# Two heads' attention scores side by side in the matmul array, in two passes

## The chip, the cores and the metric

The kernel runs on one core of one Trainium2 chip. The metric is device time in microseconds of one execution. A core has five engines with queues of their own: PE (TensorE, the 128 x 128 matmul array, whose weight loads the profile lists as PEld), DVE (VectorE), ACT (ScalarE), POOL (GpSimd) and SP (SyncE, which here only issues DMAs). Engines wait for one another through semaphores. Matmuls write to PSUM, which the kernel uses as eight banks of 128 x 512 float32.

## The reference

The input has 2048 tokens of 448 numbers, 16 heads of 28. Two attention layers work on the same input, and a gate per token mixes them. Layer A is linear attention with learned features. Layer B is full softmax attention, and its core is what the change touches:

```python
scores = jnp.einsum("bhqd,bhkd->bhqk", q, k) * scale
p = _softmax(scores, axis=-1)
o = jnp.einsum("bhqk,bhkd->bhqd", p, v)
...
return g * a + (1 - g) * b
```

## The kernel before

Layer A and all projections fill the first third of the time. The change lies in the rest, the attention of layer B from line 810 on.

**Precision.** Queries and keys are each split into a high part, rounded to the format F32R, and a low part, what the rounding left (`keep_qk`, line 568). Both lie in DRAM. A score is the sum of four products: high with high, high with low, low with high, low with low.

**Stacks.** `load_stack` (line 822) lays these parts over the 128 rows of a tile in four blocks of 32 rows. For queries the blocks hold the parts high, high, low, low; for keys high, low, high, low. One matmul over 128 rows then gives all four products at once. A tile has four heads side by side along its columns, so a stack is 128 x 4 x 512. Each block's rows 4 to 31 hold the 28 numbers of a head. Row 0 is used for the maximum: keys have −1 there, queries the row maximum of the scores (`load_nm`, line 832), so that the matmul gives score minus maximum, and ScalarE can take the exponential directly. There are two query stacks and five key stacks; `stack` (line 815) fills them once on POOL.

**Steps.** Heads come in four groups g of four, queries in four blocks qb of 512, keys in 16 tiles kt of 128. The loop from line 1094 makes 256 steps s, 16 for each pair of g and qb. A step has, in this order on PE:

- `scores(s, 0)` and `scores(s, 1)` (line 844): four matmuls st, one for each head, into a PSUM bank each; ScalarE makes p = exp(st) from each (line 868)
- `values(s - 1)` (line 970): the product of the p of the step before with the values, in four column strips of 32 (eight matmul instructions, pv)
- `mx_visit()` (line 304): a visit of the search for row maxima of later blocks. Four matmuls pm on 28 rows each, in four row strips; ScalarE copies one of them (rl, line 325) and frees its bank, DVE reduces the others (lines 329 and 332)

The visits end after about 212 steps. From then on a block also has four projections of finished output (`project`, line 982).

**Banks.** One bank belongs to pv; seven go round in the list `free`. After the scores, line 872 puts the banks back in an order that mixes those that ScalarE empties with those that DVE empties. The bank of rl goes in last (line 916), and so the fourth score of the next step takes it.

**DMA.** The order on PE, DVE, ACT and POOL is that of the program. SP's order is set by a scheduler. At kt = 12 of a block the program loads queries and maxima of the next (lines 1103 to 1106), and new keys in the last block of a group. `finish` (line 1014) normalizes a block: the denominators go out to DRAM and back (denb, rdb, rsb), POOL multiplies, and the result is stored (od). In the last block `load_out` (line 930) reads into a key stack that is no longer used.

Of the kernel before, what the change touches and what calls it, by code (L numbers as in the profile page):

```python
# [9 lines left out]
F32R = mybir.dt.float32r  # L10
# [7 lines left out]
P = 128  # L18
# [3 lines left out]
DH = 28  # L22
GW = 112
NG = 4
# [10 lines left out]
def f32(ap):  # L35
    return ap.bitcast(F32)
# [3 lines left out]
def gated_mix_kernel(ctx, tc, xT, wqkB, wvB, wvA, wkAT, wqAT, phi, woA, woB,  # L40
# [7 lines left out]
    nc = tc.nc  # L48
# [18 lines left out]
    def ps_mx(nm, d):  # L67
        return ps.tile([P, 2, 512], F32, tag="md" if d and psn[1] == 3 else "mx", name=nm,
                       bufs=1 if d and psn[1] == 3 else 2)
# [6 lines left out]
    q_d = [qk_d[g * GW:(g + 1) * GW] for g in range(NG)]  # L76
    k_d = [qk_d[D + g * GW:D + (g + 1) * GW] for g in range(NG)]
# [628 lines left out]
    for i in range(2 * NT + 11):  # L706
        t, q = i, i - NT
# [102 lines left out]
    at = ctx.enter_context(tc.tile_pool(name="at", bufs=1, side="right", reuse_waits="tile"))  # L810
    qst_of, kst_of = {}, {}
# [1 line left out]


    def stack(nm, keys):
        r = at.tile([P, 4, 512], F32R, name=nm)
        nc.gpsimd.memset(f32(r), 0.0)
        if keys:
            nc.gpsimd.memset(f32(r[0:1]), -1.0)
        return r  # L820

    def load_stack(r, src, c, parts):
        for b, i in enumerate(parts):
            nc.sync.dma_start(f32(r[32 * b + 4:32 * b + 32]),
                              src[:, i, c:c + 512].rearrange("(j d) n -> d j n", d=DH))
        return r

    def load_q(gq):
        g, qb = divmod(gq, NQ)
        qst_of[gq] = load_stack(qst[gq % 2], q_d[g], qb * 512, (0, 0, 1, 1))  # L830

    def load_nm(gq):
        nm = nm_of.pop(gq)
        row = f32(qst_of[gq][0:1].rearrange("p a (t b r) -> p (a t) b r", b=4, r=32))
        for b in range(4):
            nc.sync.dma_start(row[:, :, b, :], nm[32 * b:32 * b + 16, :])

    def load_k(g, kb):
        kst_of[(g, kb)] = load_stack(kst[(4 * g + kb) % 5], k_d[g], kb * 512, (0, 1, 0, 1))

    NS = NG * NQ * NT
    pv_of, pts, late, mids = {}, {}, {}, {}
# [1 line left out]
    def scores(s, i):  # L844

        gq, kt = divmod(s, NT)
        g, qb = divmod(gq, NQ)

        def score(j, st):
            nc.tensor.matmul(st, kst_of[(g, kt // 4)][:, j, (kt % 4) * P:(kt % 4 + 1) * P],  # L850
                             qst_of[gq][:, j, :], start=True, stop=True)

        if s == 0:
            p = at.tile([P, 2, 512], F32, name=f"p{s}_{i}")
            st = ps_mx(f"st{s}_{i}", i)
            for jl in range(2):
                score(2 * i + jl, st[:, jl, :])
            nc.scalar.activation(p, st, AF.Exp, scale=SCALE)
            pts.setdefault(s, []).extend([p[:, 0, :], p[:, 1, :]])
            return  # L860
        sts = []
        for j in (2 * i, 2 * i + 1):
            used.append(free.pop(0))
            sts.append(bank(used[-1], f"st{s}_{j}"))
            score(j, sts[-1])
        for st in sts:
            p = late_p.tile([P, 512], F32, tag="p", name=f"p{s}_{len(pts.get(s, []))}", bufs=8)
            nc.scalar.activation(p, st, AF.Exp, scale=SCALE)  # L868
            pts.setdefault(s, []).append(p)
        if i == 1:  # L870
            a, m = used[:], held[:]
            free.extend([a[0], m[0], a[1], m[1], a[2], a[3], m[2]] if m else a)
            used.clear()
            held.clear()

    qst = [stack("qst0", False)]
    kst = [stack(f"kst{i}", True) for i in range(5)]
    qst.append(stack("qst1", False))
    stg = at
    load_q(0)  # L880
    load_nm(0)
    ps_s_.close()
    ps = ps_s_.enter_context(tc.tile_pool(name="psv", bufs=1, space=PSUM, reuse_waits="tile"))
# [4 lines left out]
    for t in range(8, NT):  # L888


        if t < NT - 1:
            value_b(t, lambda i: mx_unit() if (11 * (t - 8) + i + 1) * rest // 77
                    > (11 * (t - 8) + i) * rest // 77 else None)
        else:
            value_b(t, lambda i: scores(0, i // 3 - 1) if i in (4, 7) else None)
        take_acts()
        if t in (8, 12):
            load_k(0, t // 12)
# [12 lines left out]
    def bank(i, nm):  # L911
        return ps2.tile([P, 512], F32, tag=f"g{i}", name=nm, bufs=1)
# [17 lines left out]
    def load_out(qb):  # L930


        if qb < NQ - 1:
            o = late_p.tile([P, NG - 1, 2, 512], F32R, tag="oL", name=f"oL{qb}", bufs=1)
            oL_of[qb] = [o[:, b] for b in range(NG - 1)]
        else:
            o = kst[(4 * NG) % 5]
            oL_of[qb] = [o[:, 0:2], o[:, 2:4],
                         late_p.tile([P, 2, 512], F32R, tag="oLl", name="oLl", bufs=1)]
        tt = slice(qb * 512, (qb + 1) * 512)  # L940
        for b in range(2):
            nc.sync.dma_start(f32(oL_of[qb][b]), o_d[b * P:(b + 1) * P, :, tt])
        r = oL_of[qb][2]
        for i in range(2):
            nc.sync.dma_start(f32(r[:80, i, :]), o_d[256:336, 0, tt])
        nc.sync.dma_start(f32(r[80:, 0, :]), o_d[288:336, 1, tt])
        nc.sync.dma_start(f32(r[80:96, 1, :]), o_d[288:304, 1, tt])
        nc.sync.dma_start(f32(r[96:, 1, :]), o_d[256:288, 1, tt])
# [145 lines left out]
    for s in range(NS + 16):  # L1094
        take_acts()
        if s < NS:
            gq, kt = divmod(s, NT)
            g, qb = divmod(gq, NQ)
            if s in (0, 3):
                load_k(0, 2 + s // 3)  # L1100
            if g + 1 < NG and qb == NQ - 1 and kt % 4 == 2:
                load_k(g + 1, kt // 4)
            if kt == 12 and gq + 1 < NG * NQ:
                load_q(gq + 1)
            if kt == (12 if gq + 1 < 14 else 14) and gq + 1 < NG * NQ - 1:
                load_nm(gq + 1)
            if s in OUTS:
                load_out(OUTS.index(s))
            if g == NG - 1 and kt == 8:
                load_acc(qb)  # L1110
            if s:
                scores(s, 0)
                scores(s, 1)
# [15 lines left out]
        if NG * NQ - 1 in nm_of and NG * NQ - 1 in qst_of:  # L1129
            load_nm(NG * NQ - 1)  # L1130
# [70 lines left out]
```

## Time and profile before

| what | value |
|---|---|
| runs | 1028.19 and 1028.88 us, median 1028.54 |
| span of the profiled execution | 1027.1 us |
| its own time | one of the two runs, 1.1 or 1.8 us over the span |
| PE busy | 1018.7 us, 99% |
| ACT busy | 819.4 us, 80% |
| DVE busy | 672.8 us, 65% |
| st matmuls | 1024, 315.6 us busy |
| pv matmuls | 2048, 272.8 us busy |
| pm matmuls in visits | 848, 107.1 us busy |
| DMA queue of the program | 97.74 MB, 35.4% of 16 engines |
| clock granted to PE | 0.998 of full |

The span runs from the first to the last instruction of the core. "Busy" is the union of an engine's instructions. Matmuls are pipelined: the next one begins before the one before has ended, so durations of neighbours overlap: what a matmul costs is the distance between starts. The same holds for ScalarE. In the timeline a row gives start, length, engine, line, operation, tiles and count, with merged neighbours in one row, and in brackets the idle time before it and what ended it.

### The profile page before, as it was taken

The numbers are of one execution on the slowest core, as the hardware profiler recorded it, in microseconds if no ns is written. First come the engines' busy times: TensorE is split into PE (matmuls) and PEld (weight loads), VectorE is DVE, ScalarE is ACT, GpSimd is POOL, SyncE is SP. The second block draws the span as 40 slices with busy tenths as digits, with TensorE's granted clock in tenths as the row PEclk, the third lists the DMA queues.
The fourth block names the chain that finished last, engine by engine and source line by source line (L and its number), as shares of the span: only waits on it lengthen the run. The fifth ranks groups of instructions, "written<-read, shape, count | busy, mean of one in ns | idle before, by whom it ended". The sixth has DMA issues, their size and how long they took to land.

```text
span 1027.1 us, 17751 instructions
## 1 busy us (share of the span) xinstructions
PE 1018.7 (99%) x6344; PEld 561.2 (55%) x6344; DVE 672.8 (65%) x1335; ACT 819.4 (80%) x1534; POOL 245.1 (24%) x213
## 2 busy tenths in 40 slices
PE   8999999999999999999999999999999999999998
PEld 7878888878779433333333333333333333354545
DVE  5466566997750578888878788787878887710102
ACT  5354445687753899999999999999999999969672
POOL 1226456688436302111011110101201101011010
PEclk9999999999999999999999999999999999999999
DMA  8873110132245703233633123522313355414311
GB/s 294 292 243 116 42 34 19 43 90 79 91 129 122 158 19 83 65 71 68 127 70 77 46 66 81 129 57 50 87 46 74 87 131 138 124 56 127 122 42 54
DMA packets 64025, 98.88 MB, mean 96 GB/s; under 512 B 17952, under 2 KB 24720, under 8 KB 63936
## 3 DMA queue, kind: packets, MB, share of 16 engines
q1 hardware_dynamic: 63936, 97.74, 35.4%
q8 instruction: 50, 0.82, 0.4%
q14 instruction: 39, 0.32, 0.1%
HBM read 69.54 MB, written 27.78 MB: 95 GB/s over the span
## 4 chain that ended last, share of the span: by engine, by line
PE 95%; DVE 2%; DMA 1%; ACT 1%; issue 0%; SPq 0%; DVEq 0%; ACTq 0%
PE st L850 29%; PE pv L977 25%; PE pm L321 9%; PE pqk L108 5%; PE poa L108 4%; PE pk L126 4%; PE pva L126 4%; PE pob L108 3%; PE pq L108 3%; PE pvb L108 2%; PE pmb L284 2%; PE pvb L126 2%; PE pn L532 1%; PE pft L520 1%; PE pkv L475 1%; PE poL L1011 1%
## 5 line engine op out<-in xcount | busy, mean ns | idle before, releaser
L868 ACT ACTIVATE p<-st 128x512 f32<-128x512 f32 x1020 | 525.9, 609 | 29.5 <-PE st L850 27.8
L332 DVE TENSOR_REDUCE part<-pm 128x1 f32<-128x512 f32 x477 | 304.6, 685 | 131.5 <-PE pm L321 124.9
L850 PE MATMUL st<-qst,kst 128*128 128x512 f32 x1024 | 315.6, 430 | 0.5 <-ACT vb L694 0.5
L977 PE MATMUL pv<-p,vb 128*32 128x512 f32 x2048 | 272.8, 605 | 0.2 <-DVE oUb L398 0.2
L850 PEld LDWEIGHTS st<-qst,kst 128*128 128x128 f32 x1024 | 173.1, 187 | 137.4 <-issue 75.8
L321 PEld LDWEIGHTS pm<-kc,qc 28*128 28x128 f32 x848 | 40.5, 181 | 177.8 <-ACT p L868 169.4
L325 ACT ACTIVATE rl<-pm 128x512 f32<-128x512 f32 x212 | 126.9, 599 | 11.1 <-PE pm L321 0.3
L419 POOL TENSOR_TENSOR oUb<-oUb,rsb 128x512 f32<-128x512 f32 x15 | 19.4, 1291 | 469.2 <-DMA rsb<-rdb 375.1
L329 DVE CUSTOM_DVE_ANT_0 rl<-pm,rl 128x512 f32<-128x512 f32 x159 | 108.2, 680 | 0.0
L321 PE MATMUL pm<-kc,qc 28*128 28x512 f32 x848 | 107.1, 495 | 0.0
L289 DVE CUSTOM_DVE_ANT_0 rl<-pmb,rl 128x512 f32<-128x512 f32 x88 | 57.1, 686 | 32.4 <-ACT rl L287 32.4
L977 PEld LDWEIGHTS pv<-p,vb 128*32 128x32 f32 x2048 | 40.3, 108 | 67.6 <-issue 63.4
L988 DVE SCALAR_TENSOR_TENSOR acc<-pob,gate,acc 128x448 f32<-128x448 f32 x12 | 8.2, 683 | 86.2 <-PE pob L108 86.2
L108 PE MATMUL pqk<-XH,wB 128*128 128x512 f32 x192 | 60.8, 404 | 2.3 <-DVE ev L572 2.3
L287 ACT ACTIVATE rl<-pmd 128x1024 f32<-128x1024 f32 x44 | 45.3, 1029 | 8.0 <-ACT z_s L485 2.4
L571 ACT CAST ev<-pqk 128x512 fp32r<-128x512 f32 x28 | 16.0, 589 | 40.2 <-PE pqk L108 35.7
L108 PE MATMUL poa<-woA_s,oTa 128*128 128x448 f32 x192 | 43.2, 374 | 0.0
L108 PEld LDWEIGHTS pqk<-XH,wB 128*128 128x128 f32 x192 | 36.0, 192 | 11.4 <-DVE ev L572 2.7
L572 DVE TENSOR_TENSOR ev<-pqk,ev 128x512 fp32r<-128x512 f32 x28 | 19.0, 690 | 31.6 <-ACT ev L571 31.5
L108 PEld LDWEIGHTS poa<-woA_s,oTa 128*128 128x128 f32 x192 | 35.0, 188 | 5.8 <-issue 2.8
L195 POOL TENSOR_TENSOR kc<-kc,kd 28x512 fp32r<-28x512 f32 x12 | 15.4, 1282 | 95.7 <-DMA kc<-qkd 59.4
L126 PE MATMUL pk<-wkA_s,XH 128*128 128x448 f32 x128 | 37.9, 377 | 0.0
(155 smaller groups left out, 1186.6 us busy)
## 6 DMA issues: line engine op xcount, KB each, us to landing
qkd<-ev SPq DMA_DIRECT2D x28, 512.0 KB
qst<-qkd SPq DMA_DIRECT2D x64, 224.0 KB
kst<-qkd SPq DMA_DIRECT2D x64, 224.0 KB
od<-oTb SPq DMA_DIRECT2D x48, 112.0 KB
rsa<-rda SPq DMA_DIRECT2D x8, 512.0 KB
rsb<-rdb SPq DMA_DIRECT2D x15, 256.0 KB
kc<-qkd SPq DMA_DIRECT2D x64, 56.0 KB
gad<-ga SPq DMA_DIRECT2D x16, 224.0 KB
```

Source lines behind the costliest of these rows:

```text
L108: nc.tensor.matmul(dst, l, r, start=i == 0, stop=i == len(todo) - 1)
L126: nc.tensor.matmul(dst[:, :n], l, r, start=i == 0, stop=i == len(todo) - 1, skip_group_check=True)
L284: nc.tensor.matmul((pb if j < 2 else pd)[:, j % 2, :], qc[js, qt * P:(qt + 1) * P], kc[js, :], start=True, stop=True, tile_position=(32 * ...
L287: nc.scalar.activation(rl, pd, AF.Relu)
L289: nc.vector.tensor_tensor_reduce(rl[:, i, :], pb[:, i, :], rl[:, i, :], 1.0, LOWEST, ALU.add, ALU.max, part[:, col + i:col + i + 1])
L321: nc.tensor.matmul(pm[j], mxs[("qc", gq)][js, qt * P:(qt + 1) * P], mxs[("kc", g, kb)][js, :], start=True, stop=True, tile_position=(32 * ...
L325: nc.scalar.activation(rl, pm[kb], AF.Relu if kb < 3 else AF.Copy)
L329: nc.vector.tensor_tensor_reduce(r, pm[j], r, 1.0, LOWEST, ALU.add, ALU.max, part[:, col + j:col + j + 1])
L332: nc.vector.tensor_reduce(part[:, col + j:col + j + 1], pm[j], AX.X, ALU.max)
L850: nc.tensor.matmul(st, kst_of[(g, kt // 4)][:, j, (kt % 4) * P:(kt % 4 + 1) * P], qst_of[gq][:, j, :], start=True, stop=True)
L868: nc.scalar.activation(p, st, AF.Exp, scale=SCALE)
L977: nc.tensor.matmul(pv[32 * j:32 * j + 32, :], vb[kt // 8][:, kt % 8, 4 * g + j, :], pt[j], start=kt == 0, stop=kt == NT - 1, tile_position ...
```

## The change

The array is split into two halves of 64 rows, and two heads work at the same time, one in each half. The blocks of 32 rows now hold, for keys: high and low part of the pair's first head, high and low part of its second. For queries all four blocks hold one part, and a second set of columns the other: `[:, pair, 0, :]` has the high parts and `[:, pair, 1, :]` the low ones. A score is the sum of two passes, high then low part of the queries, against the same keys, accumulated in the head's bank. A pair is issued as: pass 0 of both heads, pass 1 of both heads.

So a step has eight score matmuls on 64 rows for four on 128, each with its own weight load. Key stacks shrink from 128 x 4 x 512 to 128 x 2 x 512, query stacks keep their size. Keys are loaded with as many DMAs as before, of half the size; queries with eight DMAs for four, of half the size each; the maxima with sixteen DMAs of 4 rows for four DMAs of 16, since they now go to row 0 and row 64 and to pass 0 alone. ScalarE's reads of a pair follow both of its passes. The last block's output has a tile of its own in place of a key stack.

```diff
     def stack(nm, keys):
-        r = at.tile([P, 4, 512], F32R, name=nm)
+        r = at.tile([P, 2, 512] if keys else [P, 2, 2, 512], F32R, name=nm)
         nc.gpsimd.memset(f32(r), 0.0)
         if keys:
-            nc.gpsimd.memset(f32(r[0:1]), -1.0)
+            for e in (0, 64):
+                nc.gpsimd.memset(f32(r[e:e + 1]), -1.0)
         return r
...
+    def half(src, i, c, e):
+        return src[:, i, c:c + 512].rearrange("(p e d) n -> e d p n", e=2, d=DH)[e]

     def load_q(gq):
         g, qb = divmod(gq, NQ)
-        qst_of[gq] = load_stack(qst[gq % 2], q_d[g], qb * 512, (0, 0, 1, 1))
+        qst_of[gq] = r = qst[gq % 2]
+        for b in range(4):
+            for i in range(2):
+                nc.sync.dma_start(f32(r[32 * b + 4:32 * b + 32, :, i, :]),
+                                  half(q_d[g], i, qb * 512, b // 2))

     def load_nm(gq):
         nm = nm_of.pop(gq)
-        row = f32(qst_of[gq][0:1].rearrange("p a (t b r) -> p (a t) b r", b=4, r=32))
+        for e in range(2):
+            for p in range(2):
+                row = f32(qst_of[gq][64 * e:64 * e + 1, p, 0, :]).rearrange(
+                    "o (t b r) -> o t b r", b=4, r=32)
+                for b in range(4):
+                    at_row = 32 * b + 8 * p + 4 * e
+                    nc.sync.dma_start(row[:, :, b, :], nm[at_row:at_row + 4, :])
+
+    def load_k(g, kb):
+        kst_of[(g, kb)] = r = kst[(4 * g + kb) % 5]
         for b in range(4):
-            nc.sync.dma_start(row[:, :, b, :], nm[32 * b:32 * b + 16, :])
-
-    def load_k(g, kb):
-        kst_of[(g, kb)] = load_stack(kst[(4 * g + kb) % 5], k_d[g], kb * 512, (0, 1, 0, 1))
+            nc.sync.dma_start(f32(r[32 * b + 4:32 * b + 32]),
+                              half(k_d[g], b % 2, kb * 512, b // 2))
...
-        def score(j, st):
-            nc.tensor.matmul(st, kst_of[(g, kt // 4)][:, j, (kt % 4) * P:(kt % 4 + 1) * P],
-                             qst_of[gq][:, j, :], start=True, stop=True)
+        def pair(sts):
+            for x in range(2):
+                for e in range(2):
+                    rows = slice(64 * e, 64 * e + 64)
+                    nc.tensor.matmul(
+                        sts[e], kst_of[(g, kt // 4)][rows, i, (kt % 4) * P:(kt % 4 + 1) * P],
+                        qst_of[gq][rows, i, x, :], start=x == 0, stop=x == 1,
+                        tile_position=(64 * e, 0), skip_group_check=True)
...
         for j in (2 * i, 2 * i + 1):
             used.append(free.pop(0))
             sts.append(bank(used[-1], f"st{s}_{j}"))
-            score(j, sts[-1])
+        pair(sts)
...
-            o = kst[(4 * NG) % 5]
+            o = at.tile([P, 4, 512], F32R, name="oLs")
```

More of the change, by code (lines that the diff above doesn't have):

```diff
@@ L815, in stack @@
     def stack(nm, keys):
-        r = at.tile([P, 4, 512], F32R, name=nm)
+        r = at.tile([P, 2, 512] if keys else [P, 2, 2, 512], F32R, name=nm)
         nc.gpsimd.memset(f32(r), 0.0)
         if keys:
-            nc.gpsimd.memset(f32(r[0:1]), -1.0)
-        return r
[L822 to L826, printed above, removed]
+            for e in (0, 64):
+                nc.gpsimd.memset(f32(r[e:e + 1]), -1.0)
+        return r
+    def half(src, i, c, e):
+        return src[:, i, c:c + 512].rearrange("(p e d) n -> e d p n", e=2, d=DH)[e]
     def load_q(gq):
         g, qb = divmod(gq, NQ)
-        qst_of[gq] = load_stack(qst[gq % 2], q_d[g], qb * 512, (0, 0, 1, 1))
+        qst_of[gq] = r = qst[gq % 2]
[3 more added lines that the diff above has]
+                                  half(q_d[g], i, qb * 512, b // 2))
     def load_nm(gq):
         nm = nm_of.pop(gq)
-        row = f32(qst_of[gq][0:1].rearrange("p a (t b r) -> p (a t) b r", b=4, r=32))
+        for e in range(2):
[7 more added lines that the diff above has]
+        kst_of[(g, kb)] = r = kst[(4 * g + kb) % 5]
         for b in range(4):
-            nc.sync.dma_start(row[:, :, b, :], nm[32 * b:32 * b + 16, :])
-    def load_k(g, kb):
-        kst_of[(g, kb)] = load_stack(kst[(4 * g + kb) % 5], k_d[g], kb * 512, (0, 1, 0, 1))
+            nc.sync.dma_start(f32(r[32 * b + 4:32 * b + 32]),
+                              half(k_d[g], b % 2, kb * 512, b // 2))
     NS = NG * NQ * NT
@@ L855, in scores @@
             st = ps_mx(f"st{s}_{i}", i)
-            for jl in range(2):
-                score(2 * i + jl, st[:, jl, :])
+            pair([st[:, jl, :] for jl in range(2)])
             nc.scalar.activation(p, st, AF.Exp, scale=SCALE)
```

## The prediction

> **What bounds the kernel now.** I read the page first, for the engine that carries the end.
>
> ```profile
> span 1027.1 us, 17751 instructions
> ...
> PE 1018.7 (99%) x6344; PEld 561.2 (55%) x6344; DVE 672.8 (65%) x1335; ACT 819.4 (80%) x1534; POOL 245.1 (24%) x213
> ...
> PE 95%; DVE 2%; DMA 1%; ACT 1%; issue 0%; SPq 0%; DVEq 0%; ACTq 0%
> ...
> L868 ACT ACTIVATE p<-st 128x512 f32<-128x512 f32 x1020 | 525.9, 609 | 29.5 <-PE st L850 27.8
> ...
> L850 PE MATMUL st<-qst,kst 128*128 128x512 f32 x1024 | 315.6, 430 | 0.5 <-ACT vb L694 0.5
> ...
> L321 PE MATMUL pm<-kc,qc 28*128 28x512 f32 x848 | 107.1, 495 | 0.0
> ```
>
> TensorE carries 95% of the chain. The pm row counts 848 matmuls, four per visit: of the 256 attention steps, 212 also carry a visit of the maximum search. The other steps, near the end, have none. The two kinds must be costed apart, so I took the timeline of one step of each. First a step with a visit:
>
> ```profile
> 701.93 0.51 PE L321 MATMUL pm<-kc,qc 28*128 28x512 f32 x4
> ...
> 702.36 1.25 PE L850 MATMUL st<-qst,kst 128*128 128x512 f32 x4
> ...
> 702.46 0.60 ACT L325 ACTIVATE rl<-pm 128x512 f32<-128x512 f32 x1
> ...
> 702.96 2.06 ACT L868 ACTIVATE p<-st 128x512 f32<-128x512 f32 x4
> 703.11 0.19 PEld L850 LDWEIGHTS st<-qst,kst 128*128 128x128 f32 x1 [0.22 <-ACT rl L325]
> ...
> 703.54 1.06 PE L977 MATMUL pv<-p,vb 128*32 128x512 f32 x8
> ...
> 704.53 0.51 PE L321 MATMUL pm<-kc,qc 28*128 28x512 f32 x4
> ```
>
> From pm to the next pm is 704.53 − 701.93 = 2.60 us. The reader is to see that this is a loop through two engines, not PE at work without pause. pm ends, and 0.53 us after its start ScalarE begins rl. rl takes 0.60. The fourth weight load of the scores starts 0.05 after rl ends, because the fourth score writes the bank that rl empties. From there it is 0.43 to pv and 0.99 to the next pm. 0.53 + 0.60 + 0.05 + 0.43 + 0.99 = 2.60, the whole period. ScalarE is not the bound, though it looks busy throughout: four p in 2.06 us start every (2.06 − 0.60) / 3 = 0.49 us, so five fill about 2.45 of 2.60. The view of waits tells how general this is:
>
> ```profile
> PEld st L850 <- ACT rl L325: 46.1, 212, 0.2
> ...
> PEld pm L321 <- ACT p L868: 169.4, 202, 0.8
> ```
>
> The first row is that wait, once in each of the 212 visits. The second is larger and misleads: PE is still streaming pv in those 0.8 us, as it does in a step without a visit, where pv takes the same 1.00 us. A step without a visit, and the scores of the one before it in pairs:
>
> ```profile
> 985.07 0.73 PE L850 MATMUL st<-qst,kst 128*128 128x512 f32 x2
> ...
> 985.41 0.63 PE L850 MATMUL st<-qst,kst 128*128 128x512 f32 x2
> ...
> 987.19 1.19 PE L850 MATMUL st<-qst,kst 128*128 128x512 f32 x4
> ...
> 988.31 1.07 PE L977 MATMUL pv<-p,vb 128*32 128x512 f32 x8
> ```
>
> Here PE alone sets the pace: scores 1.12 us, pv 1.00 (from 986.19 to 987.19 in the step before). A score matmul starts about 0.23 after the one before it (0.63 less a last duration near 0.40). The first gap is 0.34, because the first weight load of a section is not covered: 0.11 more.
>
> **The change, part by part.** *Scores.* Four full-array matmuls per step become eight, each on 64 rows, two side by side: four passes. Side-by-side row strips are in the trace: the four pm matmuls on 28 rows each take 0.43 us from start to the next section, where one after the other would need 0.9. Passes of several column strips back to back are in it too:
>
> ```profile
> 216.27 1.95 PE L532 MATMUL pn<-fT,KV 112*64 112x256 f32 x16
> ...
> 216.53 1.22 PEld L532 LDWEIGHTS pn<-fT,KV 112*64 112x64 f32 x12
> ```
>
> Sixteen matmuls in pairs are eight passes; with the last lasting about 0.38, seven gaps of (1.95 − 0.38) / 7 = 0.22 us, and the loads of the later pairs run beside them. These are float32 matmuls over 256 columns, which go through the array twice, so they stream as long as 512 columns of scores. A pass of two scores thus costs 0.22 (this row) to 0.23 (the score row); I take 0.225.
>
> Without a visit, four passes take the place of four matmuls: three gaps of 0.225 for three of 0.235, −0.03 us in 43 steps = **−1.3 us** (ends 0 and −2.5). ScalarE starts one pass later there, because both scores of a pair end together; pv of the next step, 2 us later, covers it.
>
> With a visit the order matters. The matmul that needs rl's bank was the fourth of four. Now it is in the third pass, and its head needs a fourth pass after it. The other head's passes can go on, but that gains nothing: after rl, the blocked head still needs both of its passes, where one was left before. rl itself depends on pm, so it does not come earlier. The term of 0.43 becomes 0.43 + 0.225, and the period 2.83. ScalarE's 2.45 fits in that. 212 x 0.225 = **+47.7 us** (ends 0.21 x 205 = 43 and 0.235 x 212 = 49.8).
>
> *The start of the scores.* The query load becomes eight DMAs for four, the load of the maxima sixteen for four; both stand ahead of the first keys in SP's queue.
>
> ```profile
> 323.44 1.65 SPq L824 DMA_DIRECT2D qst<-qkd  x4
> 325.13 2.53 SPq L836 DMA_DIRECT2D qst<-nm  x4
> 327.76 9.42 SPq L824 DMA_DIRECT2D kst<-qkd  x13
> ...
> 336.88 0.39 PEld L850 LDWEIGHTS st<-qst,kst 128*128 128x128 f32 x2
> ...
> SPq L413 <- DMA rdb<-denb: 12.5, 12, 3.9
> ```
>
> SP spends (325.13 − 323.44) / 4 = 0.42 us per query DMA and (327.76 − 325.13) / 4 = 0.66 per DMA of maxima. Eight and sixteen take 3.4 + 10.6 us, so the first key DMA moves from 327.76 to 337.4, the fourth is out at 339.1, and with 1.0 us to land (12.5 / 12, the last row, of small DMAs) it is there at 340.1. PE loaded the first keys at 336.88: **+3.2 us** of idle PE. The ends are 0, if the smaller DMAs issue in 0.4, and 5. That key loads are halved saves nothing where SP's issue, not the bytes, is last.
>
> *Every later block of queries.* Sixteen more DMAs, four of queries and twelve of maxima, are 4 x 0.42 + 12 x 0.66 = 9.6 us of SP in a block of 16 steps. SP has room:
>
> ```profile
> SPq L401 <- DVE part L332: 101.9, 13, 15.3
> ...
> SPq L1034 <- POOL oTb L428: 71.6, 10, 9.5
> ...
> 699.25 2.48 SPq L836 DMA_DIRECT2D qst<-nm  x4
> ...
> 712.79 1.26 PE L850 MATMUL st<-qst,kst 128*128 128x512 f32 x4
> ```
>
> It waits for other engines for over 170 us in these two rows alone. In the order of the changed kernel at most the last six maxima stay behind the stores of od; 6 x 0.66 from 699.25 is 703.2, and the block that needs them starts at 712.79. So I cost this at nothing. Behind them stand the denominators' DMAs (denb, rdb, rsb), up to 9 us later; their reader is POOL, and the projection that needs it is ten steps on. If that cover is gone it costs a few us in each of the last three blocks.
>
> *Waits on DMA.* PE's first scores of a block now carry up to 17 semaphore waits for about five.
>
> ```profile
> L850 PEldq EVENT_SEMAPHORE  x79: 51/51/763, 334.8 to 966.6; - x79
> ```
>
> Each is an instruction of 51 ns; 17 are 0.87 us, most of it passed while pv streams. I take 0.17 us in each of 15 blocks, **+2.5 us** (ends 0 and 13).
>
> *The rest.* Memory of the key stacks halves, their fills on POOL with it, and the last block's inputs get a tile of their own; all of this runs ahead of SP or off the chain: 0.
>
> The sum: 47.7 + 3.2 + 2.5 − 1.3 = **+52.1 us** on a span of 1027.1. The two times shown lie 1.1 and 1.8 above the span. On the median of 1028.5 this gives **1081 us**, 5.1% slower.
>
> **Rivals.** *The wait does not close the loop.* If rl were ready before the third pass, PE alone would set the step: 0.43 + 1.09 + 1.00 = 2.52 for 2.60, −0.08 x 212 = −17, with the other terms −12: 1016 us. It decides where rl ends 0.23 us earlier against the scores than in the step shown. The count of 212 waits speaks against it.
>
> *Loads are not covered.* The second pass loads weights into rows that are streaming. If that load had to wait, each gap would be 0.34, as the first gap shows: 0.115 more in 212 steps and 3 x 0.11 more in 43, 24 + 14 us: 1119. The covered loads of pn speak against it, though those strips are columns. The Trainium skill, page "TensorE: Matmul & The Clock Gate", Part 3 on row and column tiling, says that loads overlap running matmuls only where their row group differs (its Part 2 also lets a load into a background buffer run ahead). By the narrow rule this rival would hold; the trace does not bear it out for full-row loads: the later st loads here hide in gaps of 0.23.
>
> *The pairs do not run side by side,* so the change does not do what it says. Eight passes in a row make the scores four gaps of 0.235 longer, 0.94 in 43 steps and, as PE and no longer rl is then last, about 0.9 in the 212: +231, so 1260 us. The four pm matmuls in 0.43 speak against it.
>
> *Faster by over 2%* needs the step to fall by 0.1 us net of 5 us of new waits; no row offers it but the first rival at its far end.
>
> **How the numbers follow.** The forecast has 0.79; uncovered loads 0.07; serial pairs 0.03; the loop open 0.08; something faster than that 0.03. About 2% is what a measurement of this kernel can tell from no change: below 1008 or above 1049. Slower: 0.79 + 0.07 + 0.03 = 0.89. Same: 0.08. Faster: 0.03. The forecast's own ends are 43 − 2.5 = +41, so 1069, and 49.8 + 5 + 13 = +68, so 1097. That range holds the likeliest case and little else, about 8 in 10, and I keep it.
>
> **What will show it.** The step with a visit: 2.8 us, its scores section 1.4, the wait for rl before the sixth score load, rl 0.1 after the scores' start as before. The step without: 2.1. PE idle near 337 us for about 4 us, released by a DMA. The two matmuls of a pass start within some ns. I am wrong if the step with a visit stays at 2.6 (the loop was not it), goes to 2.95 (uncovered loads) or beyond 3 (serial pairs), or if blocks begin with idle PE behind a DMA.

## The result and the profile after

The changed kernel takes 1087.44 us (1087.01 and 1087.87), against 1028.54 before: ratio 1.0573, with an interval of 1.0542 to 1.0603. That is 6.4 us above the 1081.0 predicted, inside the range of 1069 to 1097. The profiled execution has a span of 1086.1 us, so 59.0 more than before, where the sum said 52.1. First the page of the kernel after:

```profile
span 1086.1 us, 20917 instructions
...
PE 1074.0 (99%) x7368; PEld 592.1 (55%) x7368; DVE 673.2 (62%) x1335; ACT 842.2 (78%) x1534; POOL 241.5 (22%) x218
...
PE 94%; DVE 2%; SPq 2%; DMA 2%; ACT 0%; issue 0%; ACTq 0%; DVEq 0%
...
L862 PE MATMUL st<-qst,kst 64*128 64x512 f32 x2048 | 369.4, 436 | 3.9 <-POOL qst L817 3.1
```

PE's busy time grew by 55.3 us and the st row by 53.8. But 2048 matmuls of 436 ns in 369.4 us do not tell in which steps the time was lost. Cut at the first score of a step, the two traces compare like this (us):

| stretch | before | after | difference |
|---|---|---|---|
| up to the first score | 337.08 | 338.53 | +1.45 |
| steps 0 to 2 | 8.17 | 14.20 | +6.04 |
| steps 3 to 213 | 549.57 | 598.81 | +49.24 |
| steps 214 to 254 | 114.05 | 116.26 | +2.21 |
| last step and end | 18.27 | 18.28 | +0.01 |

**A step with a visit**, in the timeline of after (start, length, engine, line, operation, tiles, count, and in brackets the idle time before and what ended it):

```profile
744.23 0.51 PE L321 MATMUL pm<-kc,qc 28*128 28x512 f32 x4
744.66 0.53 PEld L862 LDWEIGHTS st<-qst,kst 64*128 64x128 f32 x5 [0.24 <-issue]
744.66 1.47 PE L862 MATMUL st<-qst,kst 64*128 64x512 f32 x8
744.75 0.60 ACT L325 ACTIVATE rl<-pm 128x512 f32<-128x512 f32 x1
...
745.40 0.29 PEld L862 LDWEIGHTS st<-qst,kst 64*128 64x128 f32 x3 [0.21 <-ACT rl L325]
...
746.07 1.06 PE L990 MATMUL pv<-p,vb 128*32 128x512 f32 x8
...
747.06 0.51 PE L321 MATMUL pm<-kc,qc 28*128 28x512 f32 x4
```

The loop is still there, with one longer link. rl starts 0.52 after pm, takes 0.60, and 0.05 later the sixth of the eight weight loads starts: five loads, a wait, three loads. From there it is 0.67 to pv, where it was 0.43, and 0.99 to the next pm: 2.83 in all. The median of the steps 3 to 213 went from 2.606 to 2.838 us. The view of waits of after (who waited for whom: us in total, times, longest) has the wait as often as before:

```profile
PEld st L862 <- ACT rl L325: 46.3, 212, 0.2
```

**A step without a visit,** from the same timeline near the end:

```profile
1038.95 1.20 PE L862 MATMUL st<-qst,kst 64*128 64x512 f32 x8
...
1040.08 1.07 PE L990 MATMUL pv<-p,vb 128*32 128x512 f32 x8
...
1041.08 1.20 PE L862 MATMUL st<-qst,kst 64*128 64x512 f32 x8
```

From scores to pv it is 1.13 us, from scores to scores 2.13; the median of such steps is 2.12 in both kernels. So pairs do run side by side, and four passes cost what four full matmuls cost. In this step the two matmuls of a pass start within 4 ns of each other. The second pass starts 0.34 behind the first, the others 0.23 apart, like single score matmuls before.

**The start of the scores.** In the timeline of after, SP's queue and PE:

```profile
321.61 3.37 SPq L831 DMA_DIRECT2D qst<-qkd  x8
...
325.02 9.98 SPq L842 DMA_DIRECT2D qst<-nm  x16
...
335.10 7.41 SPq L847 DMA_DIRECT2D kst<-qkd  x16
```

```profile
335.05 0.37 PE L126 MATMUL pvb<-wvB_s,XH 128*128 128x448 f32 x1
338.53 0.54 PE L862 MATMUL st<-qst,kst 64*128 64x512 f32 x1 [3.11 <-POOL qst L817]
339.81 1.19 PE L862 MATMUL st<-qst,kst 64*128 64x512 f32 x3 [0.74 <-DMA kst<-qkd]
340.93 0.74 PE L126 MATMUL pvb<-wvB_s,XH 128*128 128x448 f32 x1
341.47 0.57 PE L126 MATMUL pvb<-wvB_s,XL 128*128 128x448 f32 x1
```

The sixteen DMAs of maxima hold SP for 10 us; the first keys go out at 335.10 and PE stands idle for 3.11 us, then for another 0.74. POOL is named as what ended the first idle time, with a fill of a query stack. But that fill is of the second stack, which step 0 does not read, and in the run with fewer DMAs below the first score starts at 336.08, ahead of the same fill at 337.45. What came last were the keys. The first score reads rows 0 to 63, so the first two key DMAs; they are out at 335.10 + 2 x 0.46 = 336.0, and the score starts 2.5 us later. The second head's two are out at 336.95, and its score starts 2.9 us later. The first stretch of the table is only 1.45 longer all the same, because PE came to the gap 1.8 us sooner than before (last pvb row at 335.05, before at 336.88).

What the reader should not pass over is the length of the rows behind it: 0.74 and 0.57 us for pvb matmuls that took 0.37 before the gap. The table of windows of after (stretch, length, busy time of PE, PEld, DVE, ACT and POOL with the number of instructions, then the granted clock, the DMA share and GB/s) says why:

```profile
338.00:341.00 3.00, 1.72 (x5) 0.75 (x5) 0.00 (x0) 0.00 (x0) 1.75 (x2) 0.63 0.93 201
341.00:344.00 3.00, 3.00 (x9) 1.76 (x9) 0.00 (x0) 1.41 (x2) 0.00 (x0) 0.50 0.96 206
...
349.00:352.00 3.00, 3.00 (x28) 1.12 (x20) 1.89 (x3) 1.93 (x4) 0.00 (x0) 1.00 0.36 65
```

After the idle time the granted clock fell to half, and it was full again only from 349.0. With the wait for the second keys, this is the +6.04 in steps 0 to 2; the run that fills the gap, below, tells the two apart.

**The last steps** lost 0.8 us in each of the three blocks that have projections: 0.2 in three of the four steps with one (4.36 to 4.56), 0.1 in the first of them and 0.1 in the step behind the last. The others lost nothing. Weight loads before, then after:

```profile
906.97 0.59 PEld L108 LDWEIGHTS pob<-woB_s,oTb 128*128 128x128 f32 x3
907.58 0.85 PEld L850 LDWEIGHTS st<-qst,kst 128*128 128x128 f32 x4
```

```profile
963.70 0.59 PEld L108 LDWEIGHTS pob<-woB_s,oTb 128*128 128x128 f32 x3
964.60 0.76 PEld L862 LDWEIGHTS st<-qst,kst 64*128 64x128 f32 x8 [0.31 <-issue]
```

Before, the first score load ran beside the last matmul of the projection, 0.02 behind the last load. After, it stands back 0.31, and it starts only when the last matmul of the projection (963.90 + 0.77) is all but through. Three such blocks make 2.4 us; one plain step that was 0.2 longer before (2.35) takes that much back, which leaves the 2.21.

### The profile page after: what moved, and what is told of

The parts are those of the page before. It is cut to its first block, busy times and chain, and to the rows that moved or that the text cites. A ratio compares the mean times of both kernels' runs of the same rounds, so it can differ in the third digit from the quotient of the medians.

```text
span 1086.1 us, 20917 instructions
## 1 busy us (share of the span) xinstructions
PE 1074.0 (99%) x7368; PEld 592.1 (55%) x7368; DVE 673.2 (62%) x1335; ACT 842.2 (78%) x1534; POOL 241.5 (22%) x218
## 4 chain that ended last, share of the span: by engine, by line
PE 94%; DVE 2%; SPq 2%; DMA 2%; ACT 0%; issue 0%; ACTq 0%; DVEq 0%
PE st L862 32%; PE pv L990 24%; PE pm L321 8%; PE pqk L108 5%; PE poa L108 4%; PE pk L126 4%; PE pva L126 3%; PE pob L108 3%; PE pq L108 3%; PE pvb L108 2%; PE pmb L284 2%; PE pn L532 1%; PE pft L520 1%; SPq L842 1%; PE pkv L475 1%; PE poL L1024 1%
## 5 line engine op out<-in xcount | busy, mean ns | idle before, releaser
L862 PE MATMUL st<-qst,kst 64*128 64x512 f32 x2048 | 369.4, 436 | 3.9 <-POOL qst L817 3.1
L862 PEld LDWEIGHTS st<-qst,kst 64*128 64x128 f32 x2048 | 205.2, 185 | 137.6 <-issue 83.4
L108 PE MATMUL pq<-wqA_s,XH 128*128 128x448 f32 x128 | 37.4, 374 | 0.0
```

What stands on the lines that cost most here:

```text
L108: nc.tensor.matmul(dst, l, r, start=i == 0, stop=i == len(todo) - 1)
L862: nc.tensor.matmul(sts[e], kst_of[(g, kt // 4)][rows, i, (kt % 4) * P:(kt % 4 + 1) * P], qst_of[gq][rows, i, x, :], start=x == 0, stop=x == 1,
```

## The experiments

My theory: the visit step is the loop through rl's bank, and pairs cost only because two passes instead of one follow that wait. The rival that I took most seriously: pairs of 64 rows are slower by themselves where PE changes between tile shapes, and the wait is only where it shows. A third cause, SP's issue of small DMAs, would sit at the start alone.

**One bank to spare, with pairs and without.** The visit does three pm matmuls instead of four, so that one of the seven banks is always free. This leaves out one head's maximum in every visit, and its reduction reads another head's bank.

```diff
-        b = [free.pop(0) for _ in range(4)]
+        b = [free.pop(0) for _ in range(3)]
         free.append(b[0])
...
-            for j in sorted(range(4), key=lambda j: j != kb):
+            for j in sorted(pm, key=lambda j: j != kb):
...
-            free.extend([a[0], m[0], a[1], m[1], a[2], a[3], m[2]] if m else a)
+            free.extend([m[0], a[0], m[1], a[1], a[2], a[3]] if m else a)
...
```

On the kernel after:

> The changed kernel, with three matmuls in a visit in place of four, so that a bank of PSUM comes free and no score waits for the bank that ScalarE's rl empties. Left out: the maximum of one head in each visit; DVE reduces another head's bank again in its place, so its work is the same. Theory (the loop pm, rl, blocked score, pv): the wait on rl is gone, a step with a visit falls from 2.84 to PE's own sum, 0.43 + 1.13 + 1.00 = 2.56 us, and the time by 212 x 0.28 = 59 to about 1028 us. Rival (eight score matmuls are themselves longer on PE than four): the step stays near 2.84 and the time at 1087.

On the kernel before:

> The same free bank in the kernel before, with the same maximum left out. Theory: its step of 2.60 holds 0.05 us of waiting for rl, so it falls to 2.55 and the time by 11 to about 1018 us. The distance to e1 is then what the change costs beside the loop: about 7 us at the start of the scores and 2 in the projections. Rival (PE has no pause in the step before): 2.60 and 1028.

The pairs took 1028.56 us, ratio to the unchanged kernel before 0.9986 (0.9975 to 0.9998); the kernel before with the same edit 1017.55, ratio 0.9882 (0.9867 to 0.9896). The median steps are 2.554 and 2.550 us. The timeline of the pairs with a spare bank:

```profile
747.96 0.51 PE L321 MATMUL pm<-kc,qc 28*128 28x512 f32 x3
...
748.39 0.76 PEld L863 LDWEIGHTS st<-qst,kst 64*128 64x128 f32 x8 [0.25 <-issue]
748.59 0.63 ACT L325 ACTIVATE rl<-pm 128x512 f32<-128x512 f32 x1
...
749.52 1.06 PE L992 MATMUL pv<-p,vb 128*32 128x512 f32 x8
...
750.51 0.50 PE L321 MATMUL pm<-kc,qc 28*128 28x512 f32 x3
```

Eight loads without a break, the scores in 1.13, and PE alone sets the step: 0.43 + 1.13 + 0.99 = 2.55. Without the wait, the median steps of pairs and of full matmuls differ by 0.004 us. What stays between the two spans, 1025.8 − 1016.1 = 9.7 us, is 5.6 up to step 3, 2.5 in the last steps and 1.6 in the 211 between. Three pm matmuls instead of four do not shorten the step by themselves: they run side by side, and it is 0.43 from pm to scores either way.

**rl's bank one place earlier in the kernel before.** The third score takes it, so that two matmuls follow the wait, as two passes do in the pairs. One line; nothing else changes, and nothing is left out.

```diff
-        free.append(b[0])
+        free.insert(2, b[0])
```

> The kernel before with one number changed: the bank that rl empties goes to the third score of the next step in place of the fourth. Nothing is added or left out. Theory: after rl two score matmuls are left for one, as in the changed kernel, so the step goes from 2.60 to 2.84 and the time to 1028 + 212 x 0.23 = 1077 us. Rival (the loop is not what sets the step): 2.60 and 1028.

It took 1078.21 us, ratio 1.047 (1.0449 to 1.0491), with a step of 2.840. The view of waits has the same 212 and twice the time:

```profile
PEld st L850 <- ACT rl L325: 95.7, 212, 0.5
```

The main term of the loss comes out of the old kernel, with full-array matmuls, by moving one bank: the steps 3 to 213 take 599.33 us here and 598.81 with the pairs. Together with the two runs before, where the wait was taken away and pairs and full matmuls cost the same, this leaves the pairs' shape no part in the main term.

**The same line in the kernel after.** There the third and the fourth bank belong to the two heads of one pair, so it should not matter which of them waits.

> The changed kernel with the one number of the third run: rl's bank goes to the third score of the next step, which is now the other head of the same pair. Theory (what counts is the passes left after rl, and both heads of a pair have two): no change, 2.84 and 1087 us. Rival (the place in the order of matmuls counts): another 0.1 to 0.23 in 212 steps, 1108 to 1136.

It took 1090.51 us, ratio 1.0607 (1.0586 to 1.0628). The median step is 2.842, against 2.838: the place within a pair does not matter. The profiled span is 4.2 us longer than that of the kernel after. Of this, 2.8 are in the steps 3 to 213: 0.16 to 0.18 in the first step of 13 blocks (3.00 to 3.02 each), where I had expected none, and about 0.004 in the rest. Which wait makes those thirteen stays open. The other 1.4 lie before the first score (339.97 for 338.53), where the two kernels have the same program, so they are a difference between executions.

**One pass only.** The kernel after with the first pass alone, so one pass follows the wait. The low part of the queries is left out of every score.

```diff
-            for x in range(2):
+            for x in range(1):
...
-                        qst_of[gq][rows, i, x, :], start=x == 0, stop=x == 1,
+                        qst_of[gq][rows, i, x, :], start=True, stop=True,
```

> The changed kernel with the first pass alone. Left out: the products with the low part of the queries. Theory (after rl one pass is left, as before the change): a step with a visit goes back to 2.60, not lower, though PE has half the score work; a plain step is then bound by ScalarE's four exponentials, near 1.95. In all 1087 - 49 - 10 = 1028 us. Rival (PE's score work is what counts): both kinds of steps fall by two passes, 0.46: 2.38 and 1.66, and the time to about 970.

It took 1027.58 us, ratio 0.999 (0.998 to 1.0). Its visit step in the timeline:

```profile
746.47 0.51 PE L321 MATMUL pm<-kc,qc 28*128 28x512 f32 x4
746.91 0.29 PEld L862 LDWEIGHTS st<-qst,kst 64*128 64x128 f32 x3 [0.25 <-issue]
...
747.65 0.18 PEld L862 LDWEIGHTS st<-qst,kst 64*128 64x128 f32 x1 [0.45 <-ACT rl L325]
748.08 1.07 PE L990 MATMUL pv<-p,vb 128*32 128x512 f32 x8
```

Half of the score work of the kernel after is gone, and the step is 2.608 us, what it was in the kernel before. One pass went from behind the wait and brings 0.23; the other went from in front of it and brings nothing, since PE now waits 0.45 for rl where it waited 0.21. A step without a visit has no such wait and did get shorter, to 1.96.

**The small DMAs alone,** in the kernel before: eight query DMAs and sixteen of maxima per block, everything else as it was.

> The kernel before with the changed kernel's number of DMAs alone: queries in eight for four, maxima in sixteen for four. Theory (SP's issue time delays the first keys, PE idles, and its clock then falls to half): PE idle for 3 to 5 us before the first score, a granted clock near 0.5 for some 9 us, in all 7 to 10 us: 1036 to 1038. Keys are not halved here, so a little more than the 7 of the changed kernel. Steps stay at 2.60. Rival (the first scores wait for POOL's fills or cost more because they are paired): no idle, 1028.

It took 1048.7 us (four runs from 1045.68 to 1053.7, the profiled one 1051.02), ratio 1.0182 (1.0142 to 1.0222), 11 us beyond what I expected. The start behaved: the first score came at 343.95 instead of 337.08, and half a clock followed, +9.3 in all. Most of the rest, 11.3 us by the steps' starts, is at the three changes of head group, which I had costed at nothing; another 1.3 is at the start of a later block. SP and PE at the first change, in the timeline:

```profile
505.54 10.00 SPq L839 DMA_DIRECT2D qst<-nm  x16
...
514.89 1.02 PE L853 MATMUL st<-qst,kst 128*128 128x512 f32 x2 [1.16 <-ACT rl L325]
516.12 1.06 PE L853 MATMUL st<-qst,kst 128*128 128x512 f32 x2 [0.21 <-DMA qst<-nm]
```

All sixteen maxima are issued behind the stores of od, and the last goes out at 515.5, when PE has come to the block that needs them. The last row names that DMA; the one above it names rl, which had long ended (its copy starts at 513.75 and takes 0.60). The window behind it shows that the clock has a part here too:

```profile
517.00:521.00 4.00, 4.00 (x17) 1.57 (x16) 2.00 (x4) 2.04 (x5) 0.00 (x0) 0.57 0.87 199
```

The same is in the windows at the two other changes (0.57 and 0.58). In the kernel after the scheduler put queries and most maxima ahead of the stores, and steps at a change of group are like the others. So the cover that the prediction named (SP has room) was there only by SP's order.

**Fewer DMAs of maxima in the pairs.** The query stack is laid out pass before pair, so eight DMAs of eight rows do for sixteen of four; the row maxima are reduced in the matching order.

```diff
...
-                nc.sync.dma_start(f32(r[32 * b + 4:32 * b + 32, :, i, :]),
+                nc.sync.dma_start(f32(r[32 * b + 4:32 * b + 32, i, :, :]),
...
-                    at_row = 32 * b + 8 * p + 4 * e
-                    nc.sync.dma_start(row[:, :, b, :], nm[at_row:at_row + 4, :])
+                at_row = 32 * b + 8 * e
+                nc.sync.dma_start(row[:, :, b, :], nm[at_row:at_row + 8, :])
...
```

> The changed kernel with eight DMAs of maxima per block for sixteen: query stacks are laid out pass before pair and the maxima transposed in another order, which costs DVE one more small reduction per block. Nothing is left out. Theory (at the start of the scores SP's issue time is last): 5 us less of issue bring the first keys in before PE is there, so no idle and no slow clock: the first three steps return to the 8.2 us of before, 6 to 9 us less than the changed kernel, 1079 to 1081 us. Steps with a visit stay at 2.84. Rival (the first scores wait for POOL's fill of the second query stack, which the trace names as releaser): the idle stays, 1087.

It took 1080.7 us, ratio 1.0511 (1.0495 to 1.0527). SP needs 5.47 us for the maxima, the first score comes at 336.08, and step 3 starts at 345.29, where it started at 345.25 in the kernel before and at 352.73 after: the whole +7.5 of the start is gone. The granted clock stays at 1.00 throughout.

**The gap filled.** The kernel after with 16 matmuls of the identity into the first score's bank, so that PE is not idle while it waits for the keys.

```diff
+            if i == 0:
+                for _ in range(16):
+                    nc.tensor.matmul(st[:, 0, :P], ident, ident, start=True, stop=True)
```

> The changed kernel with sixteen float32 matmuls over 128 columns of the identity ahead of the first scores, written to a bank that the scores then overwrite. They last some 3.5 us, as long as PE idled there. Theory (the half clock of some 9 us after the gap is the answer to idle PE): the granted clock stays at 1.0, the first three steps cost only the gap, about 4 to 6 us less than the changed kernel: 1081 to 1083 us. Rival (the clock falls for another reason, or only the wait counts): no gain, 1087 or more.

It took 1085.51 us, ratio 1.056 (1.0542 to 1.0578), and the profiled span is 1083.2, less of a gain than expected. Its timeline (each filling matmul counts twice there) and its windows:

```profile
335.42 3.73 PE L872 MATMUL st<-ident 128*128 128x128 f32 x32
339.21 0.47 PE L862 MATMUL st<-qst,kst 64*128 64x512 f32 x1
340.59 0.70 PE L862 MATMUL st<-qst,kst 64*128 64x512 f32 x3 [0.91 <-DMA kst<-qkd]
```

```profile
338.00:341.00 3.00, 2.03 (x15) 1.45 (x13) 0.00 (x0) 0.00 (x0) 1.91 (x2) 1.00 0.77 220
```

The clock stays full. Steps 0 and 1 take 4.48 + 3.25 us for 6.76 + 4.61 in the kernel after, 3.64 less. The filling ran 0.68 too long (first score at 339.21, not 338.53), so step 3 starts only 3.0 us sooner, and PE still waits 0.91 for the second keys. So of the 7.5 us at the start the clock has 3.0 to 3.6, and the rest is the wait for keys. That idle PE is what brings the half clock is borne out by the other pairs: the four traces with this gap have it, those without the gap (fewer DMAs, the filled gap, the visit ahead of pv below) do not.

**The visit ahead of pv.** All this points to putting other PE work between pm and the score that needs rl's bank. pv is such work. The visit moves between the scores and pv of a step, and the banks go round in another order. Nothing is left out.

```diff
-            free.extend([a[0], m[0], a[1], m[1], a[2], a[3], m[2]] if m else a)
+            free.extend(m + a)
...
+        if s:
+            mx_visit()
         if 0 < s <= NS:
             values(s - 1)
             if s % NT == 0:
                 finish(s // NT - 1, s)
-        if s:
-            mx_visit()
```

On the kernel before:

> The kernel before, with the visit (four pm matmuls, rl and the reductions) put between the scores and pv of its step instead of behind pv, and the banks handed round so that pm takes the banks of the last visit's three other heads and of the step's first p. Nothing is left out. rl then runs while pv streams, and the score that takes its bank comes 1.4 us after pm, not 0.7. If the loop through rl sets the step, it falls to what PE alone needs, 0.43 + 1.12 + 1.00 = 2.55 us as with one bank to spare, so 1028.5 - 0.055 x 212 = 1017 us. Rival: ScalarE (2.45 us of every step) or the reductions on VectorE (2.0 us from pm's end, whose last bank pm now needs back after 2.55 us) take rl's place as what PE waits for; then the step stays at 2.60 or grows, 1028 us or more.

On the pairs with fewer DMAs:

> The pairs with eight DMAs of maxima per block, and the same edit: the visit between scores and pv. Nothing is left out. If the pairs cost only because two passes follow the wait for rl, the step falls from 2.84 to about 2.56 and the time from 1080.7 by 0.28 x 212 = 59 to about 1021 us. If pairs cost something in the visit steps by themselves, or the rival of the run beside this one holds (ScalarE starts a pair's p one pass later, so it has less slack), the step stays above 2.6 and the time above 1030 us.

The kernel before took 1030.03 us, ratio 1.0011 (1.0001 to 1.002), the pairs 1094.37, ratio 1.0633 (1.0617 to 1.0649): the rival held both times. In neither is there a wait for rl among the larger ones any more, and the steps are 2.612 and 2.900 us. The timeline of the first:

```profile
702.83 0.57 PE L321 MATMUL pm<-kc,qc 28*128 28x512 f32 x4
...
703.40 1.29 DVE L332 TENSOR_REDUCE part<-pm 128x1 f32<-128x512 f32 x2 [0.66 <-PE pm L321]
...
704.61 0.68 DVE L329 CUSTOM_DVE_ANT_0 rl<-pm,rl 128x512 f32<-128x512 f32 x1
...
705.45 0.24 PEld L321 LDWEIGHTS pm<-kc,qc 28*128 28x128 f32 x4 [0.36 <-DVE part L329]
```

Now pm takes back the bank of the last reduction: 0.57 to the reductions, 1.89 for three, 0.16 to the next pm, 2.62. One loop went, and another of the same length took its place. In the pairs it is ScalarE:

```profile
702.56 1.27 PE L863 MATMUL st<-qst,kst 64*128 64x512 f32 x8
703.39 2.07 ACT L882 ACTIVATE p<-st 128x512 f32<-128x512 f32 x4 [0.34 <-PE st L863]
703.76 0.78 PE L323 MATMUL pm<-kc,qc 28*128 28x512 f32 x4
704.47 1.06 PE L991 MATMUL pv<-p,vb 128*32 128x512 f32 x8
```

The first p starts 0.83 us after the scores, 0.54 in the kernel without pairs, since it needs both passes. It ends at 703.98, and pm, which takes its bank, gets three of its four matmuls away only at 704.04: pm to pv is 0.71 instead of 0.50. From the scores to that p 0.83, p 0.60, to pm 0.05, to pv 0.43, to the next scores 0.99: the 2.90 of the step. So pairs have a second price, which the order of the kernel after hides: their results come late. No run here that leaves nothing out was faster than the kernel before.

## Why the prediction was right, and where not

**The loop (+47.7): right, in size and place.** Steps 3 to 213 gained 49.24 for 211 steps, 0.233 each, where 0.225 was taken; the low end of 0.21 can go. The path is the one that was forecast: the wait before the sixth load, rl 0.1 after the scores' start. The rival that the loop is open (1016) falls with the 212 waits and with the run that frees a bank.

**Steps without a visit (−1.3): the term mis-sized, with the wrong sign.** The plain step is unchanged, and the blocks with projections lost 0.8 us each, +2.2 in all. The prediction counted gaps inside the section of scores and overlooked its edge: after a projection the first load had been covered.

**The start of the scores (+3.2): the largest miss, +7.5.** The cause of the idle time was right: keys that stand behind 24 DMAs. Its size (3.11 us, and 0.74 for the second keys) came out near 3.2 by luck. SP began 1.8 us sooner than in the kernel before (321.61 for 323.44) and needed 0.62 us for a DMA of maxima instead of 0.66, but the keys took 2.5 to 2.9 us to land, where 1.0 was taken from small DMAs. What failed is the step "the idle time is the price". Its second part is the half clock after it, worth 3.0 to 3.6 us. The trace of before has a small case of it, early in the projections, which the prediction did not use (a row of the timeline, then a window):

```profile
23.04 1.01 PE L108 MATMUL pqk<-XH,wB 128*128 128x512 f32 x2 [2.29 <-DVE ev L572]
...
23.00:26.00 3.00, 2.96 (x8) 2.29 (x9) 0.69 (x1) 0.56 (x1) 0.00 (x0) 0.55 0.91 307
```

The +7.5 is uncertain by some 1.5 us: in the pairs with rl's bank moved, whose start of the scores has the same half clock, step 3 starts at 354.20, and 1.4 of that 1.5 had passed before the first score.

**Waits on DMA (+2.5): nearly nothing.** The waits are there; the profile counts 167 at the score line for 79. But the steps that begin a block are not longer; only three steps in all show 0.12 us more. So nearly all of these waits pass beside other work.

**SP in later blocks (0): right here, by SP's order.** The prediction gave two reasons, that SP has time to spare and that at most six maxima stay behind the stores in the order of the changed kernel. Only the second holds: the kernel before with small DMAs has the first as well, and lost 11.3 us at the changes of group.

**Loads not covered (1119) and pairs in a row (1260)** fall with the plain step: 2.12 us, passes 0.23 apart. The narrow rule that the prediction weighed (the Trainium skill, page "TensorE: Matmul & The Clock Gate", Part 3) does not hold in this trace: in the plain step above the loads of the second pass start at 1039.06 for rows whose first pass streams from 1038.96 to 1039.45, and they hide.

The sum by measured terms: 7.5 + 49.2 + 2.2 = 58.9, on 1027.1. The misses of the small terms partly cancel: the start and the last steps cost 7.8 us more than forecast, the waits on DMA 2.5 less.

## What to carry to other kernels

When a step is a loop through a buffer that another engine empties, only the work behind the wait counts: find the matmul that waits, and count what a change puts behind it. Reordering moves that wait to the next buffer in turn, so list what each engine hands back and when before spending effort on it. And many small DMAs ahead of a first load cost the issue time on their queue, plus what an idle PE loses in clock: look for idle PE in the trace at hand, and at the granted clock behind it, before costing a new gap.

## What the runs showed of the hardware

- The half clock comes in multiples of about 3.4 us, worked out from the mean clock of the windows around it: 3.4 near 23 us in the kernel before and at each change of group in the kernel before with small DMAs, 6.8 at the start of the scores in the pairs with a spare bank, 10.2 there in the kernel after (338.8 to 349.0), 13.6 with one pass only. The Trainium skill, page "TensorE: Matmul & The Clock Gate", Part 1, puts the throttle in after an idle window of about 3.4 us and out after a busy one of the same length, with windows that run free of the kernel. The length agrees with these traces. That one busy window is enough does not: in the kernel after, PE is busy throughout from 341.0, and the clock stays at half until 349.0.
- The length of the idle time alone does not decide whether the clock falls. Near 20 us, 2.29 us of idle PE brought the half clock in the kernel before; 2.13 us in the kernel after, and 3.41 us in the kernel before with rl's bank moved, did not.
- Behind the 128-row matmuls of a projection the first load for 64 rows starts 0.31 us behind the last load, where a 128-row load starts 0.02 behind. The Trainium skill, page "TensorEngine Tiling (Array Packing)", Key Properties, says that a change of tiling mode drains the engine; here the change costs 0.2 us behind a projection.
- One DMA of four rows of maxima, 0.5 KB, holds SP's queue for 0.62 us, longer than a query DMA of 112 KB, at 0.42.
